# Sums of weights and of x from GpSimd to VectorE in a linear-attention and double-MLP kernel on one core, with later stores

## The chip, the core and the metric

One NeuronCore of a Trainium2 chip runs the whole program. Its engines are TensorE (PE: matmuls; PEld: its weight loads), VectorE (DVE), ScalarE (ACT), GpSimd (POOL) and SyncE (SP), whose queue issues nearly all DMAs here. Each engine takes its instructions in the order of its own queue and waits for the others by semaphores. The metric is the device time of one execution in microseconds (us); less is better.

## The reference

Linear attention with a normalization, then two MLPs, the first gated, the second with softplus, all in float32. The inputs arrive as float64 words.

```python
kv = np.einsum('bhsd,bhse->bhde', k, v)               # 4 x 8 heads, 576 x 64
out = np.einsum('bhsd,bhde->bhse', q, kv)
out = out / np.sqrt(np.mean(out * out, axis=-1, keepdims=True) + 1e-06) * g_norm
x = out.transpose(0, 2, 1, 3).reshape(2304, 512)
x = (x @ w_a) * (x @ w_b) @ w_out                     # 512 -> 1536 -> 512
h = x @ w_in                                          # 512 -> 2048
out = (np.maximum(h, 0) + np.log1p(np.exp(-np.abs(h)))) @ w_out2   # 2048 -> 512
```

## The kernel before

**Numbers.** Every operand of a matmul is held as two halves, a high one in the rounded format fp32r (written by ACT, `half_hi`, line 169) and the rest (written by DVE, `half_lo`, line 172); three matmuls make one product. Raw weights are loaded as pairs of 32-bit words (`w_load`, line 185) and turned into float32 in place: line 193 (DVE) and line 197 (ACT) in `w_begin`, line 202 (DVE) in `w_value`. Then `w_split` makes the two halves.

**Strassen-like products.** Behind its first third the kernel works on pairs of token blocks (of 512 tokens) with seven products in place of eight. These need sums of blocks of weights and of x. `w_sums` makes four sums from two raw tiles, into the second words of those tiles; each is 128x256, and each of the last two needs one of the first two. `x_steps` makes, for two chunks in each of two pairs of blocks, four whole tiles out of the halves (`whole`, line 692) and four sums (`plus`, line 698), all 128x512; between them `cutting` splits the results on ACT and DVE. `g_sums` (lines 935 and 936) makes sums of activations for the last layer. In the kernel before, all of these run on POOL.

**Order.** The attention and twelve slots of the first MLP are written out by hand (`SCRIPT`) and fill about the first 150 us. Behind it the program is a chain of generators; each `yield` is one *point*, mostly six matmuls of 512 columns. Work beside the matmuls is spread over points in jobs: `job_first` (weights of the first MLP for the first pair, with `w_sums`; 8 times), `job_keep` (weights of the second MLP, with `w_sums`; 16 times), `job_out`, and `job_again`, which loads back what `job_first` stored for the second pair. So `w_sums` runs 24 times and makes 96 sums. `x_steps(0)` lies beside the last slots, `x_steps(1)` beside the second half of the first pair's MLP, on tiles that `unpark` loads back from DRAM. `gated` makes the products of the first MLP, four passes of 16 points for the first pair; one pass has 14 groups of six matmuls of 512 columns and two groups of 24 of 256 columns (`first0`). The compiler may reorder what isn't in the hand-written part: an instruction that is ready may be put ahead of earlier ones on its engine.

**Stores.** Split weights that are used again go to DRAM (`keep`, line 517), raw tiles with their sums too (`drop` in `job_first`, line 629). Both are handed to `later` (line 510), which gives the store out so many points afterwards: 12 by default, 16 in `drop`. All big tiles (raw words, halves, operands) come from one pool of 39 buffers of 4 KB a partition. `park` stores the halves of x of two blocks (line 679), at points 1 and 33.

Of the kernel before, what the change touches and what calls it, by code (L numbers as in the profile page):

```python
# [13 lines left out]
ALU = mybir.AluOpType  # L14
# [98 lines left out]
def attention_gated_softplus_kernel(  # L113
# [14 lines left out]
    nc = tc.nc  # L128
# [14 lines left out]
    def t2(shape, dt=F32, what="t2"):  # L143
        return t2pool.tile(shape, dt, tag="t2", name=nm(what))
# [7 lines left out]
    def t4(shape, dt, what):  # L152
        return big.tile(shape, dt, tag="big", name=nm(what))
# [20 lines left out]
    def split(hi, lo, src):  # L174
        half_hi(hi, src)
        half_lo(hi, lo, src)
# [5 lines left out]
    def w_load(item):  # L182
        key, src = item
        t = t4([P, 512, 2], I32, "raw")
        nc.sync.dma_start(out=t, in_=src.bitcast(I32).rearrange("p (n t) -> p n t", t=2))
        raws[key] = t

    def w_begin(item, parts="AB"):
        t = raws[item[0]]
        low = t[:, :, 0]  # L190
        high_f = t.bitcast(F32)[:, :, 1]
        if "A" in parts:
            nc.vector.tensor_scalar(
                out=low, in0=low, scalar1=29, scalar2=None, op0=ALU.logical_shift_right
            )
        if "B" in parts:
            nc.scalar.activation(out=high_f, in_=high_f, func=AF.Prelu, scale=HIGH_SCALE, alpha=SIGN_SCALE)  # L197

    def w_value(item):
        t = raws[item[0]]  # L200
        low, high = t[:, :, 0], t[:, :, 1]
        nc.vector.scalar_tensor_tensor(  # L202
            out=low, in0=high, scalar=3, in1=low, op0=ALU.logical_shift_left, op1=ALU.bitwise_or
        )

    def w_split(item, word=0):
        w = t4([P, 2, 512], F32R, "w")
        split(w[:, 0], w[:, 1], raws[item[0]].bitcast(F32)[:, :, word])
        return w
# [297 lines left out]
    now = [0]  # L507
    due = []

    def later(f, points=12):  # L510
        due.append((now[0] + points, f))
        due.sort(key=lambda x: x[0])

    def keep(key, item, word=0):
        t = w_split(item, word)
        to = kept_w[key] = kept.tile([P, 2, 512], F32, name="kept_" + "_".join(map(str, key)))
        later(lambda: nc.sync.dma_start(out=to, in_=t.bitcast(F32)))
        return t
# [4 lines left out]
        return t  # L523

    def minus(to, a, b):
        nc.gpsimd.tensor_tensor(out=to, in0=a, in1=b, op=ALU.subtract)  # L526

    def w_sums(items, across):
        (l0, h0), (l1, h1) = ([raws[x[0]].bitcast(F32)[:, :, w] for w in range(2)] for x in items)
        k0, k1 = slice(0, 256), slice(256, 512)  # L530
        b11, b12, b21, b22 = l0[:, k0], l0[:, k1], l1[:, k0], l1[:, k1]
        if across:
            b12, b21 = b21, b12
        minus(h0[:, k0], b12, b11)
        minus(h1[:, k0], b22, b12)
        minus(h0[:, k1], b22, h0[:, k0])
        minus(h1[:, k1], b21, h0[:, k1])
# [81 lines left out]
    def job_first(m, fp):  # L619

        l = [((m, f), {"a": w_a, "b": w_b}[m][f]) for f in (2 * fp, 2 * fp + 1)]

        def made(k, item, word):
            w1[fp, m, k] = w_split(item, word)

        def drop(k):
            t = raws.pop(l[k][0])
            to = kept_w["f", m, fp, k] = kept.tile([P, 512, 2], I32, name=f"kept_{m}_{fp}_{k}")
            later(lambda: nc.sync.dma_start(out=to, in_=t), 16)

        return [lambda x=x: w_load(x) for x in l], [
            lambda: w_begin(l[0]),
            lambda: (w_value(l[0]), w_begin(l[1])),
            lambda: made(0, l[0], 0),
            lambda: w_value(l[1]),
            lambda: w_sums(l, True),
            lambda: made(1, l[1], 0),
            lambda: None,
            lambda: (made(2, l[0], 1), drop(0)),
            lambda: (made(3, l[1], 1), drop(1)),  # L640
        ]
# [43 lines left out]
    def x_steps(pair):  # L685
        j1, j2 = PAIRS[pair]
        r = {}

        def whole(j, kk):
            x = xhl[j, kk].bitcast(F32)  # L690
            t = r[j, kk] = t2([P, 512], what="xr")
            nc.gpsimd.tensor_tensor(out=t, in0=x[:, 0], in1=x[:, 1], op=ALU.add)

        def known(name, j, kk, k):
            ops["x", pair, name, k] = xhl.pop((j, kk))

        def plus(to, a, b, op):
            nc.gpsimd.tensor_tensor(out=to, in0=a, in1=b, op=op)

        def cutting(name, kk, src):  # L700
            t = ops["x", pair, name, kk] = t4([P, 2, 512], F32R, "op")
            split(t[:, 0], t[:, 1], src)

        def sums(kk):
            r11, r12, r21, r22 = (r.pop((j, k)) for j in (j1, j2) for k in (kk, kk + 2))
            plus(r22, r21, r22, ALU.add)
            cutting("S1", kk, r22)
            plus(r21, r11, r21, ALU.subtract)
            plus(r11, r22, r11, ALU.subtract)
            cutting("S2", kk, r11)  # L710
            cutting("S3", kk, r21)
            plus(r12, r12, r11, ALU.subtract)
            cutting("S4", kk, r12)

        def names(kk):
            known("A11", j1, kk, kk)
            known("A12", j1, kk + 2, kk)
            known("A22", j2, kk + 2, kk)
            xhl.pop((j2, kk))

        return [x for kk in range(2) for x in (
            lambda kk=kk: (whole(j2, kk), whole(j2, kk + 2)),
            lambda kk=kk: (whole(j1, kk), whole(j1, kk + 2)),
            lambda kk=kk: (sums(kk), names(kk)),
        )]
# [655 lines left out]
```

## Time and profile before

| | |
|---|---|
| median of 3 runs | 867.63 us (866.86 to 867.80) |
| the profiled execution | 868.36 us, of which the trace's span is 866.6 us |
| PE busy | 836.9 us, 97% of the span |
| DVE busy | 666.4 us, 77% |
| ACT busy | 444.3 us, 51% |
| POOL busy | 216.5 us, 25% |
| granted clock of PE, mean | 0.992 |

All times in rows count from the start of the span. A busy share is the time in which an engine executes, with whatever slows the instruction included; for PE it includes time at the lower clock. The granted clock is 1 at 2.4 GHz and 0.5 at 1.2 GHz. A wait is put down to the instruction whose end released it.

### The profile page before, as it was taken

The page shows a single profiled execution, that of the slowest core. Times are in us where ns is not written, and L with a number is a line of the kernel's source. Part 1 is how long each engine was busy: PE and PEld are TensorE (multiplying, and loading weights), DVE is VectorE, ACT ScalarE, POOL GpSimd, SP SyncE. Part 2 cuts the span into 40 slices and gives each one's busy share as a digit, 9 for nine tenths or more (in the row PEclk, how much of TensorE's full clock was granted, in tenths as well). Part 3 has the DMA queues.
Part 4 walks back from the last instruction along what each step waited for, and adds up shares of the span by engine and source line. Part 5 has one row for each costly group of instructions (what it writes and reads, how often), then busy time and mean ns, then how long its engine had stood idle before and what let it go on. Part 6 is the DMA issues. An engine that isn't in the chain of part 4 may idle for free.

```text
span 866.6 us, 12122 instructions
## 1 busy us (share of the span) xinstructions
PE 836.9 (97%) x4204; PEld 692.9 (80%) x4204; DVE 666.4 (77%) x1051; ACT 444.3 (51%) x806; POOL 216.5 (25%) x168
## 2 busy tenths in 40 slices
PE   7999999997999999899999999999999999999998
PEld 5778788886778887778877788877888888887886
DVE  3988773798988789757778956999992767697951
ACT  5799784446656465446664623336560323235630
POOL 0000000884654157411326412331000212111000
PEclk9999999999999999989999999999999999999999
DMA  9993213545877898428699997345488954425941
GB/s 287 318 250 99 93 73 122 193 179 197 284 294 274 275 365 339 167 103 269 234 406 417 344 397 291 120 141 178 160 277 315 387 186 154 146 86 181 320 167 49
DMA packets 81324, 197.92 MB, mean 228 GB/s; under 512 B 7536, under 2 KB 38768, under 8 KB 81264
## 3 DMA queue, kind: packets, MB, share of 16 engines
q1 hardware_dynamic: 81120, 197.16, 64.8%
q8 instruction: 33, 0.54, 0.3%
q14 instruction: 27, 0.22, 0.1%
q10 hardware_dynamic: 144, 0.00, 0.0%
HBM read 142.08 MB, written 55.05 MB: 227 GB/s over the span
## 4 chain that ended last, share of the span: by engine, by line
PE 69%; DVE 14%; DMA 5%; POOL 4%; ACT 4%; issue 4%; SPq 0%; DVEq 0%; POOLq 0%; ACTq 0%
PE acc L1028 17%; PE z L592 4%; PE v L592 4%; PE x L592 4%; PE a L1202 4%; PE acc L429 4%; PE b L1202 4%; DVE w L172 3%; PE acc L862 3%; PE h L1070 3%; POOL raw L526 2%; PE acc L1048 2%; PE y L592 2%; DMA raw<-in_w_out 2%; PE ya L592 2%
## 5 line engine op out<-in xcount | busy, mean ns | idle before, releaser
L1028 PE MATMUL acc<-op,w2o 128*128 128x512 f32 x672 | 153.7, 390 | 1.5 <-DVE op L172 1.5
L1028 PEld LDWEIGHTS acc<-op,w2o 128*128 128x128 f32 x672 | 125.9, 188 | 28.9 <-DVE op L172 2.8
L172 DVE TENSOR_TENSOR w<-raw,w 128x512 fp32r<-128x512 f32 x148 | 121.5, 842 | 28.0 <-ACT w L169 27.5
L526 POOL TENSOR_TENSOR raw<-raw,raw 128x256 f32<-128x256 f32 x56 | 65.7, 1179 | 269.7 <-DVE raw L202 224.9
L169 ACT ACTIVATE w<-raw 128x512 fp32r<-128x512 f32 x148 | 93.7, 670 | 57.8 <-POOL raw L526 23.1
L583 ACT ACTIVATE g<-g 128x512 f32<-128x512 f32 x64 | 39.3, 630 | 100.6 <-DVE g L580 100.5
L172 DVE TENSOR_TENSOR op<-g,op 128x512 fp32r<-128x512 f32 x96 | 63.7, 707 | 4.6 <-ACT op L169 4.5
L429 PE MATMUL acc<-ghl,w 128*128 128x512 f32 (+1 forms) x240 | 57.0, 379 | 3.6 <-ACT y L455 3.4
L197 ACT ACTIVATE raw<-raw 128x512 f32<-128x512 f32 x68 | 45.2, 679 | 29.0 <-DMA raw<-in_w_out 12.1
L862 PE MATMUL acc<-ghl,wo 128*128 128x512 f32 (+1 forms) x288 | 57.3, 357 | 2.3 <-DVE ghl L172 2.0
L169 ACT ACTIVATE op<-g 128x512 fp32r<-128x512 f32 x96 | 53.7, 622 | 8.5 <-DVE op L172 3.6
L862 PEld LDWEIGHTS acc<-ghl,wo 128*128 128x128 f32 x288 | 47.5, 189 | 12.2 <-DVE ghl L172 3.6
L526 POOL TENSOR_TENSOR raw<-raw 128x256 f32<-128x256 f32 x40 | 45.0, 1129 | 47.3 <-DVE raw L202 38.9
L935 POOL TENSOR_TENSOR s<-g 128x512 f32<-128x512 f32 x14 | 19.6, 1397 | 140.5 <-DVE g L585 133.0
L202 DVE SCALAR_TENSOR_TENSOR raw<-raw 128x512 int32<-128x512 int32 x68 | 50.0, 741 | 4.7 <-ACT raw L197 2.6
L429 PEld LDWEIGHTS acc<-ghl,w 128*128 128x128 f32 x240 | 42.5, 195 | 11.3 <-ACT y L455 3.6
L172 DVE TENSOR_TENSOR ghl<-g,ghl 128x512 fp32r<-128x512 f32 (+1 forms) x56 | 46.3, 836 | 5.4 <-ACT ghl L169 5.3
L592 PE MATMUL z<-op,w 128*128 128x512 f32 x192 | 48.9, 390 | 1.3 <-DVE c L603 1.3
L592 PE MATMUL v<-op,w 128*128 128x512 f32 x192 | 49.2, 391 | 0.0
L592 PE MATMUL x<-op,w 128*128 128x512 f32 x192 | 48.3, 389 | 0.0
L169 ACT ACTIVATE ghl<-g 128x512 fp32r<-128x512 f32 (+1 forms) x56 | 33.4, 609 | 23.1 <-DVE g L396 23.1
L862 PE MATMUL acc<-ghl,w 128*128 128x512 f32 x192 | 44.3, 391 | 0.5 <-DVE ghl L172 0.5
(151 smaller groups left out, 1668.2 us busy)
## 6 DMA issues: line engine op xcount, KB each, us to landing
w<-kept SPq DMA_DIRECT2D x80, 512.0 KB, 5.9
kept<-w SPq DMA_DIRECT2D x64, 512.0 KB, 5.8
w2o<-kept SPq DMA_DIRECT2D x112, 256.0 KB, 4.9
raw<-in_w_out SPq DMA_DIRECT2D x28, 512.0 KB, 6.7
kvraw<-in_kv SPq DMA_DIRECT2D x19, 448.0 KB, 10.5
raw<-in_w_in SPq DMA_DIRECT2D x16, 512.0 KB, 5.8
wo<-kept_wo SPq DMA_DIRECT2D x16, 512.0 KB, 9.9
raw<-in_w_a SPq DMA_DIRECT2D x12, 512.0 KB, 6.9
```

Of the source, the lines that this page charges most:

```text
L169: nc.scalar.activation(out=hi, in_=src, func=AF.Copy)
L172: engine.tensor_tensor(out=lo, in0=src, in1=hi, op=ALU.subtract)
L197: nc.scalar.activation(out=high_f, in_=high_f, func=AF.Prelu, scale=HIGH_SCALE, alpha=SIGN_SCALE)
L202: nc.vector.scalar_tensor_tensor(out=low, in0=high, scalar=3, in1=low, op0=ALU.logical_shift_left, op1=ALU.bitwise_or)
L429: nc.tensor.matmul(out=acc[j][i2][:, :n], lhsT=w[:, a, c2], rhs=g[:, c, :n], start=(opens and i == 0 and (j > 0 or i2 % 2 == 0)), stop=(cl ...
L526: nc.gpsimd.tensor_tensor(out=to, in0=a, in1=b, op=ALU.subtract)
L583: nc.scalar.activation(out=to, in_=to, func=AF.Softplus)
L592: nc.tensor.matmul(out=o, lhsT=w[:, a, (2 * k + kk) * P:(2 * k + kk + 1) * P], rhs=x[:, c, :], start=(start and kk == 0 and i == 0), stop= ...
L862: nc.tensor.matmul(out=to, lhsT=w[:, a, i2 * P:(i2 + 1) * P], rhs=x, start=(f == F0 and i == 0 and (b < 2 or i2 % 2 == 0)), stop=(f == F1 ...
L1028: nc.tensor.matmul(out=set_[where][b], lhsT=w[:, a, b * P:(b + 1) * P], rhs=x[:, c, :], start=(opens and cp == 0 and q == 0), stop=(cp == ...
L1070: nc.tensor.matmul(out=h[:, k, :], lhsT=w[:, a, kk * P:(kk + 1) * P], rhs=yhl[0, kk][:, c, :], start=(k == 0 and kk == 0 and q == 0), stop ...
L1202: nc.tensor.matmul(out=live[x, i], lhsT=wt[x, f][:, a, kk * P:(kk + 1) * P], rhs=xhl[j, kk][:, c, :], start=(kk == 0 and k == 0), stop=(kk ...
```

## The change

The sums of weights (`minus` in `w_sums`) and of x (`whole` and `plus` in `x_steps`) are made by DVE in place of POOL. Sums of activations (`g_sums`) stay on POOL. Stores of split weights are given out 20 points later in place of 12, stores of raw tiles with sums 24 in place of 16. Shapes, operands and the rest of the program are the same.

```diff
-    def later(f, points=12):
+    def later(f, points=20):
         due.append((now[0] + points, f))
         due.sort(key=lambda x: x[0])
...
     def minus(to, a, b):
-        nc.gpsimd.tensor_tensor(out=to, in0=a, in1=b, op=ALU.subtract)
+        nc.vector.tensor_tensor(out=to, in0=a, in1=b, op=ALU.subtract)
...
             to = kept_w["f", m, fp, k] = kept.tile([P, 512, 2], I32, name=f"kept_{m}_{fp}_{k}")
-            later(lambda: nc.sync.dma_start(out=to, in_=t), 16)
+            later(lambda: nc.sync.dma_start(out=to, in_=t), 24)
...
             t = r[j, kk] = t2([P, 512], what="xr")
-            nc.gpsimd.tensor_tensor(out=t, in0=x[:, 0], in1=x[:, 1], op=ALU.add)
+            nc.vector.tensor_tensor(out=t, in0=x[:, 0], in1=x[:, 1], op=ALU.add)
...
         def plus(to, a, b, op):
-            nc.gpsimd.tensor_tensor(out=to, in0=a, in1=b, op=op)
+            nc.vector.tensor_tensor(out=to, in0=a, in1=b, op=op)
```

## Rows read from the trace of the kernel before

**Rows 1.** The page: busy us of each engine, share of span, instructions.

```profile
PE 836.9 (97%) x4204; PEld 692.9 (80%) x4204; DVE 666.4 (77%) x1051; ACT 444.3 (51%) x806; POOL 216.5 (25%) x168
```

**Rows 2.** Table by stretch: length, busy us of each engine, clock, DMA share, GB/s.

```profile
150.00:300.00 150.00, 139.70 (x732) 120.02 (x731) 130.89 (x177) 84.38 (x156) 85.01 (x72) 0.98 0.66 238
300.00:372.00 72.00, 67.70 (x313) 55.88 (x313) 61.07 (x84) 36.85 (x68) 36.52 (x20) 0.97 0.73 279
372.00:510.00 138.00, 135.62 (x629) 111.86 (x628) 105.71 (x174) 78.42 (x139) 46.10 (x36) 0.99 0.83 310
```

**Rows 3.** PE's waits from 140 to 372 us: total us, times, longest.

```profile
PE xa L592 <- DVE y L603: 3.8, 1, 3.8
PE acc L429 <- ACT y L455: 3.4, 1, 3.4
PE b L1164 <- DVE g L396: 2.4, 1, 2.4
PE ya L592 <- ACT ya L614: 2.3, 2, 1.6
PE yb L592 <- ACT yb L614: 2.0, 1, 2.0
```

**Rows 4.** The chain of waits, two stretches: start us, us, what.

```profile
195.52 0.32 SPq L517
...
195.89 5.68 DMA raw<-in_w_b
...
217.99 3.38 POOL raw L526 x3
...
341.85 9.50 POOL xr L692
```

**Rows 5.** Timeline, DVE and POOL around 152 us: start us, us, engine, instruction.

```profile
151.97 0.69 DVE L202 SCALAR_TENSOR_TENSOR raw<-raw 128x512 int32<-128x512 int32 x1
...
152.58 0.42 DVE L193 TENSOR_SCALAR raw<-raw 128x512 int32<-128x512 int32 x1
...
152.89 0.86 POOL L526 TENSOR_TENSOR raw<-raw,raw 128x256 f32<-128x256 f32 x1 [150.66 <-DVE raw L202]
153.11 1.19 DVE L202 SCALAR_TENSOR_TENSOR raw<-raw 128x512 int32<-128x512 int32 x1
```

**Rows 6.** POOL's groups, 150 to 370 us: busy us, mean ns, idle before, releasers.

```profile
L526 POOL TENSOR_TENSOR raw<-raw,raw 128x256 f32<-128x256 f32 x33 | 37.1, 1127 | 217.7 <-DVE raw L202 212.2 <-DMA raw<-in_w_b 3.4 <-issue 1.9
L692 POOL TENSOR_TENSOR xr<-x 128x512 f32<-128x512 f32 x16 | 34.5, 2168 | 13.4 <-DMA x<-kept_x 7.1 <-DVE op L172 6.3
L526 POOL TENSOR_TENSOR raw<-raw 128x256 f32<-128x256 f32 x27 | 27.1, 1007 | 0.9
L698 POOL TENSOR_TENSOR xr<-xr,xr 128x512 f32<-128x512 f32 x16 | 24.5, 1529 | 0.8
```

**Rows 7.** DVE's groups of the whole span, two with both inputs in SBUF.

```profile
L476 DVE TENSOR_TENSOR s<-y,y 128x512 f32<-128x512 f32 x4 | 2.6, 682 | 0.0
L172 DVE TENSOR_TENSOR y<-y,y 128x256 fp32r<-128x256 f32 x4 | 1.4, 417 | 0.0
```

**Rows 8.** DVE's five costliest groups, 150 to 370 us.

```profile
L172 DVE TENSOR_TENSOR w<-raw,w 128x512 fp32r<-128x512 f32 x84 | 77.8, 949 | 7.6 <-ACT w L169 7.4
L202 DVE SCALAR_TENSOR_TENSOR raw<-raw 128x512 int32<-128x512 int32 x38 | 29.3, 773 | 4.1 <-ACT raw L197 2.2
L193 DVE TENSOR_SCALAR raw<-raw 128x512 int32<-128x512 int32 x38 | 22.2, 590 | 5.8 <-DMA raw<-in_w_in 2.7 <-DMA raw<-in_w_a 1.3 <-DMA raw<-in_w_b 1.0
L172 DVE TENSOR_TENSOR ghl<-g,ghl 128x512 fp32r<-128x512 f32 x21 | 21.9, 1060 | 3.2 <-ACT ghl L169 3.2
L172 DVE TENSOR_TENSOR op<-xr,op 128x512 fp32r<-128x512 f32 x16 | 13.9, 922 | 7.1 <-ACT op L169 7.1
```

**Rows 9.** SP's issues between 80 and 135 us: start us, us, instruction.

```profile
85.52 44.27 SPq L679 DMA_DIRECT2D kept_x<-x  x8
129.88 1.15 SPq L185 DMA_DIRECT2D raw<-in_w_in  x2
```

## The prediction

> **What bounds the kernel now.** I read the page first: TensorE (PE) is busy 97% of the span [rows 1], so all that any change can win is the time in which PE stands still or runs at the low clock. The table by stretch says where that is: before 150 us no work of the change exists except a few loads, from 150 to 300 us PE is busy 139.70 of 150 us, from 300 to 372 us 67.70 of 72, from 372 to 510 us 135.62 of 138 [rows 2]. Behind 510 us no instruction that moves is left. So the prize lies in 150 to 372 us: 10.3 + 4.3 = 14.6 us of idle PE. Its granted clock is 0.98 and 0.97 there, 1.00 being the level of 2.4 GHz; 0.02 x 150 + 0.03 x 72 = 5.2 us are lost to stretches at the lower level, 1.2 GHz, which lie behind the longest stalls. Together 19.8 us, and with the 2.4 idle us behind 372 us 22.2 us.
>
> PE's waits name the enders: five groups make 13.9 of the 14.6 us, and each ends with VectorE (DVE) or ScalarE (ACT), never with GpSimd (POOL) itself [rows 3]. The chain of waits shows what stood behind these two. At 195.52 us it passes through a store of line 517 on the queue of SyncE (SP), which can go only when DVE has made what is stored, and right behind it through a load of 5.68 us; at 217.99 us three POOL sums take 3.38 us; at 341.85 us one POOL sum alone takes 9.50 us [rows 4]. So POOL is 25% busy on the page [rows 1], yet its work is on the path, partly as latency, partly because it slows DVE. The second is seen in the timeline: the same DVE instruction of line 202 takes 0.69 us with POOL idle, and 1.19 us when a POOL sum has begun 0.22 us before it [rows 5].
>
> **What is removed.** In 150 to 370 us POOL executes 33 + 27 sums of weights (line 526), 16 sums of two halves of x (line 692) and 16 of x (line 698): 37.1 + 27.1 + 34.5 + 24.5 = 123.2 us of POOL [rows 6]. A further 36 sums of weights lie behind 370 us (96 in all by the code, 60 of them here). The sums of line 935 and 936 behind 510 us stay on POOL.
>
> **What is added to DVE.** The trace has no DVE instruction of exactly these sums, but near ones: 128x512 with both inputs in SBUF takes 682 ns, 128x256 takes 417 ns [rows 7]. The stride of two words in the weights' sums is the same that line 172 reads in w<-raw, so I add nothing for it. 60 x 0.417 + 32 x 0.682 = 25.0 + 21.8 = 46.8 us in 150 to 370 us. Durations of neighbours overlap a little in the records, so this is the upper end.
>
> **What DVE gets back.** With POOL quiet, the groups that it slowed fall to their undisturbed durations, 683 ns for the two-input ones of 512 columns (as 682 in [rows 7]), 0.69 us for line 202 and 0.42 us for line 193 [rows 5]. From the means [rows 8]: w 84 x (0.949 - 0.683) = 22.3 us, ghl 21 x (1.060 - 0.683) = 7.9, op 16 x (0.922 - 0.683) = 3.8, line 202 38 x (0.773 - 0.69) = 3.2, line 193 38 x (0.590 - 0.42) = 6.5. Sum 43.7 us. That these means are contention and not a property of the tiles is borne out by the group that has the same instruction elsewhere [rows 7]. So DVE gains 46.8 - 43.7 = +3.1 us: the work comes over nearly for free. Bounds: all of it back and overlapping records, a few us below zero; nothing back, +46.8 us.
>
> DVE is busy 130.89 + 61.07 = 192.0 us of these 222 us [rows 2]; with +3.1 it is 195.1 us. If all 19.8 us came back the stretch would last 202.2 us, and DVE would be 96% full. That is my reason not to count on all of it: an in-order engine at 96% still makes PE wait now and then.
>
> A page of the Trainium skill speaks against the change: "Perfetto Trace Analysis", section Optimizing Scalar/DVE Operations, holds that with a saturated DVE it may pay to give work to ScalarE or even GpSimd, which is the opposite direction. It adds that between DVE and GpSimd this might not help, as they share a read port. By its first half the time would be that of the third rival below; the means of [rows 8] side with the second half.
>
> **New waits.** The weights' sums read what DVE itself wrote one step earlier (line 202), so on DVE they wait for no one; before, POOL waited for DVE, and ACT and the stores of raw weights then for POOL. Four dependent sums last 4 x 0.417 = 1.7 us in place of 3.38 us for three. In the second pair the sums of x read tiles that come back from DRAM: POOL waited 7.1 us for those loads [rows 6]. On DVE whatever is queued behind waits too: the splits of w and ghl, and the evacuations that PE needs. Price 0 to 7.1 us, in the worst case off the gain; I take 0 to 1, since DVE there has a backlog of its own and comes later to them than POOL did.
>
> **The stores.** Line 517's stores are given out 20 points after the split in place of 12, line 629's 24 in place of 16. I take this at zero. Points seem to set a priority, not a time: the eight stores of x of line 679, four given out at point 1 and four at point 33, are all issued from 85.52 to 129.8 us, ahead of the two loads that were given out before all points [rows 9]. What can be won is that a load no longer stands behind a store that waits for DVE, as at 195.5 us [rows 4]; what can be lost is in the second rival.
>
> **The sum**, stall by stall [rows 3]. Those behind POOL work, 2.0 + 2.3 + 3.8 = 8.1 us, go, but for about 1.5 us at 369 us, where DVE has to empty PSUM banks one after the other in any case: 6.6 us. Of the two around 200 us, 2.4 + 3.4 = 5.8 us, I take half, 2.9 us: they are DVE throughput, which hardly changes, plus a late load. The clock gives back in proportion, some 0.7 x 5.2 = 3.7 us. Behind 372 us zero: 36 sums x 0.417 = 15 us come to a DVE that is busy 105.7 of 138 us [rows 2], at most 2.4 us to win and about as much to lose. Total 13.2 us. The profiled execution took 868.36 us (span 866.6); 868.36 - 13.2 = 855.2 us. Its time is 0.73 us above the median of the runs, 867.63, so for a median I say 854.4 us.
>
> **Rivals.** (1) *DVE takes the place of POOL as the limit.* At 96% it still makes PE wait as it does now in 150 to 300 us, and only the stall behind the 9.50 us sum goes, with its share of the clock: about 5 us, 862.7 us. For it: the fullness worked out above. Against: half of the waits are latency through POOL, not throughput.
>
> (2) *The stores hold buffers.* The pool has 39 big tiles, and raw weights, their splits and all operands come out of it. If points do set times, each of the 8 stores of one pass of `gated` frees its tile 8 of 16 points later, that is 4 tiles more in use. A pass has 132 matmuls, at 139.70 / 732 = 0.19 us [rows 2] 25.2 us, four passes 101 us; if tiles set the pace there, 101 x 4 / 39 = 10.3 us are lost, against about 10 us won outside these passes and in them: near 868 us, no change. Against it: in [rows 9] the order goes by what is ready.
>
> (3) *The contention doesn't come back*, because what slows DVE is another user of memory (the loads are dense in the same stretch). Then DVE has 192.0 + 46.8 = 238.8 us to do in 222: +16.8 us, 884.4 us. It decides from the point where less than 16.8 of the 43.7 us come back, 38%. Against it: line 202 in [rows 5], 0.69 or 1.19 us within two microseconds, by POOL alone.
>
> **How the numbers follow.** Forecast 0.60 (845.5 to 861 us), rival 1 0.18 (861 to 865.9), rival 2 0.09, rival 3 or a milder form of it 0.13. The range leaves out rival 3 and part of 2: low end 867.63 - 22.2 = 845.4, say 845.5; high end 866.5, just past rival 1. Faster means by over 0.2%, below 865.9 us, and slower above 869.4 us; less than that a measurement of this kernel can hardly tell from no change. Faster 0.78, same 0.09, slower 0.13.
>
> **What would show it.** Right: no POOL work between 150 and 510 us; w<-raw,w near 0.69 us in that stretch; DVE's busy time in 150 to 360 us about as before; line 592's waits for line 614 and line 603 gone or under 1 us; the clock at 1.00. Wrong: the same means near 0.9 us without POOL (rival 3); PE waiting for DVE in many places of under 1 us each (rival 1); loads of raw weights waiting longer for PE, and the stores really later in SP's order (rival 2).

## The result and the profile after

The changed kernel takes 847.21 us in the median (846.87 to 847.32, 4 runs), the kernel before 867.71 us beside it. The ratio is 0.9759 with a 95% interval of 0.974 to 0.9778: 20.5 us less, where 13.2 us were forecast. The profiled execution took 847.19 us, its span is 845.4 us. First the page, engine by engine; against [rows 1] POOL lost 167.4 us, DVE gained 2.0 us, and PE is busy for 8.2 us less with the same 4204 matmuls.

```profile
PE 828.7 (98%) x4204; PEld 688.3 (81%) x4204; DVE 668.4 (79%) x1179; ACT 444.3 (53%) x806; POOL 49.1 (6%) x40
```

The stretch that holds the moved work does the same 1670 or so matmuls in both kernels. The first row is the kernel before, the second the kernel after, in the columns of [rows 2]; the kernel after is in step with it 20 us earlier at the end.

```profile
150.00:510.00 360.00, 343.01 (x1671) 287.75 (x1670) 297.68 (x433) 199.65 (x361) 167.64 (x128) 0.98 0.74 274
```

```profile
150.00:490.00 340.00, 335.58 (x1672) 283.63 (x1671) 300.11 (x561) 200.43 (x362) 0.00 (x0) 1.00 0.79 286
```

PE's idle time in it falls from 17.0 to 4.4 us, 12.6 us less; its busy time falls by 7.4 us, and the granted clock goes from 0.98 to 1.00, the level of 2.4 GHz throughout. Together 20.0 us, nearly the whole gain. DVE is busy 2.4 us more, with 128 more instructions.

The prediction's own stretch ends at 370 us. Up to there the kernel before did 1039 matmuls, and the kernel after had done as many at 353 us:

```profile
150.00:370.00 220.00, 205.40 (x1039) 174.38 (x1038) 189.96 (x256) 121.22 (x222) 121.53 (x92) 0.98 0.69 253
```

```profile
150.00:353.00 203.00, 200.70 (x1039) 171.60 (x1038) 184.57 (x348) 121.87 (x222) 0.00 (x0) 1.00 0.76 275
```

With the 92 sums that left POOL, DVE is busy 5.4 us less, and 91% of the stretch.

PE's waits from 130 to 510 us in the kernel after, in the columns of [rows 3]:

```profile
PE vb L592 <- DVE g L617: 1.9, 2, 1.2
PE acc L862 <- DVE ghl L172: 1.0, 1, 1.0
PE ya L592 <- ACT ya L614: 0.8, 1, 0.8
PE za L592 <- DVE g L603: 0.2, 1, 0.2
PE acc L862 <- DVE g L617: 0.2, 1, 0.2
```

None of the waits of [rows 3] is left (in the kernel before they end at 198, 204, 223, 250, 276 and 369 us). No wait is over 1.2 us; the two for line 617 are new and end at 262 and 288 us, and the one for line 614 is another, at 416 us.

DVE's groups from 150 to 355 us show where its 47 us of new work went. Columns as in [rows 8]; the four rows of lines 526, 698 and 692 are the moved sums.

```profile
L172 DVE TENSOR_TENSOR w<-raw,w 128x512 fp32r<-128x512 f32 x84 | 55.5, 685 | 5.2 <-ACT w L169 5.1
L202 DVE SCALAR_TENSOR_TENSOR raw<-raw 128x512 int32<-128x512 int32 x39 | 26.7, 690 | 2.5 <-ACT raw L197 1.3
L193 DVE TENSOR_SCALAR raw<-raw 128x512 int32<-128x512 int32 x40 | 16.5, 423 | 4.2 <-DMA raw<-in_w_out 2.0 <-DMA raw<-in_w_in 1.8 <-DMA raw<-in_w_b 0.3
L172 DVE TENSOR_TENSOR ghl<-g,ghl 128x512 fp32r<-128x512 f32 x21 | 14.2, 687 | 1.2 <-ACT ghl L169 1.2
L526 DVE TENSOR_TENSOR raw<-raw,raw 128x256 f32<-128x256 f32 x33 | 13.7, 421 | 0.3
L526 DVE TENSOR_TENSOR raw<-raw 128x256 f32<-128x256 f32 x27 | 11.4, 420 | 0.1
L698 DVE TENSOR_TENSOR xr<-xr,xr 128x512 f32<-128x512 f32 x16 | 11.0, 688 | 0.2
L692 DVE TENSOR_TENSOR xr<-x 128x512 f32<-128x512 f32 x16 | 10.6, 684 | 0.0
L172 DVE TENSOR_TENSOR op<-xr,op 128x512 fp32r<-128x512 f32 x16 | 10.1, 686 | 0.0
```

The sums cost 421, 420, 688 and 684 ns, where 417 and 682 were taken from other lines: 13.7 + 11.4 + 11.0 + 10.6 = 46.7 us. The old groups w, line 202, line 193, ghl and op fell from 949, 773, 590, 1060 and 922 ns [rows 8] to 685, 690, 423, 687 and 686 ns. The sums wait for next to nothing (at most 0.3 us a group); the wait of 7.1 us for x's loads that POOL had [rows 6] has no successor.

### The profile page after: what moved, and what is told of

The parts are those of the page before. It is cut to its first block, busy times and chain, and to the rows that moved or that the text cites. A ratio compares the mean times of both kernels' runs of the same rounds, so it can differ in the third digit from the quotient of the medians.

```text
span 845.4 us, 12022 instructions
## 1 busy us (share of the span) xinstructions
PE 828.7 (98%) x4204; PEld 688.3 (81%) x4204; DVE 668.4 (79%) x1179; ACT 444.3 (53%) x806; POOL 49.1 (6%) x40
## 4 chain that ended last, share of the span: by engine, by line
PE 78%; DVE 10%; DMA 8%; ACT 2%; issue 1%; SPq 0%; DVEq 0%; ACTq 0%
PE acc L1028 18%; PE acc L862 9%; PE acc L429 5%; PE z L592 5%; PE x L592 5%; PE v L592 5%; PE a L1202 4%; PE b L1202 4%; DMA raw<-in_w_out 4%; PE h L1070 3%; PE y L592 2%; PE acc L1048 2%; DVE w L172 2%; DMA raw<-in_w_in 2%; PE a L1164 2%; PE b L1164 2%
## 5 line engine op out<-in xcount | busy, mean ns | idle before, releaser
L172 DVE TENSOR_TENSOR w<-raw,w 128x512 fp32r<-128x512 f32 x148 | 98.2, 685 | 15.8 <-ACT w L169 15.7
L202 DVE SCALAR_TENSOR_TENSOR raw<-raw 128x512 int32<-128x512 int32 x68 | 46.3, 689 | 3.0 <-ACT raw L197 1.8
L429 PEld LDWEIGHTS acc<-ghl,w 128*128 128x128 f32 x240 | 41.3, 189 | 7.4
L862 PE MATMUL acc<-ghl,w 128*128 128x512 f32 x192 | 43.7, 389 | 0.0
L592 PEld LDWEIGHTS z<-op,w 128*128 128x128 f32 x192 | 35.9, 188 | 8.9 <-DVE c L603 1.5
L592 PEld LDWEIGHTS v<-op,w 128*128 128x128 f32 x192 | 36.0, 188 | 7.5
L862 PEld LDWEIGHTS acc<-ghl,w 128*128 128x128 f32 x192 | 36.0, 188 | 7.4
L592 PEld LDWEIGHTS x<-op,w 128*128 128x128 f32 x192 | 35.9, 188 | 7.4
```

What stands on the lines that cost most here:

```text
L172: engine.tensor_tensor(out=lo, in0=src, in1=hi, op=ALU.subtract)
L202: nc.vector.scalar_tensor_tensor(out=low, in0=high, scalar=3, in1=low, op0=ALU.logical_shift_left, op1=ALU.bitwise_or)
L429: nc.tensor.matmul(out=acc[j][i2][:, :n], lhsT=w[:, a, c2], rhs=g[:, c, :n], start=(opens and i == 0 and (j > 0 or i2 % 2 == 0)), stop=(cl ...
L592: nc.tensor.matmul(out=o, lhsT=w[:, a, (2 * k + kk) * P:(2 * k + kk + 1) * P], rhs=x[:, c, :], start=(start and kk == 0 and i == 0), stop= ...
L862: nc.tensor.matmul(out=to, lhsT=w[:, a, i2 * P:(i2 + 1) * P], rhs=x, start=(f == F0 and i == 0 and (b < 2 or i2 % 2 == 0)), stop=(f == F1 ...
```

## Experiments: which part of the change

Theory: the sums are the whole change, because they slow DVE from POOL and because others wait for them there; the stores are worth nothing. Rivals: the stores let loads go earlier, or hold buffers; or one kind of sum is everything.

**The stores alone** (`e1_stores_only`), on the kernel before:

```diff
-    def later(f, points=12):
+    def later(f, points=20):
...
-            later(lambda: nc.sync.dma_start(out=to, in_=t), 16)
+            later(lambda: nc.sync.dma_start(out=to, in_=t), 24)
```

> The kernel before with the later stores alone (20 and 24 points); all sums stay on GpSimd. Theory (points only set a priority among what is ready, the stores are worth nothing by themselves): within 1.7 us of the 867.7 us of before, with PE waits of the same kind near 200, 223 and 366 us. Rival (a load no longer stands behind a store that waits for VectorE, and this is a large part of the gain): 858 us or less. Rival (stores hold buffers longer): 871 us or more, with raw loads issued later.

Measured: 866.89 us beside 868.32 us, ratio 0.9988 (0.997 to 1.0007): no difference that can be told. The waits of SP's queue from 150 to 330 us are of the same kind and size; this row names the stores that wait for the sums of weights on POOL (total us, times, longest).

```profile
SPq L629 <- POOL raw L526: 42.3, 15, 10.5
```

In the kernel before that row stood at 42.5 us for the same 15 times. Eight points more made no difference in this row, and none that can be told in the time.

**The sums alone** (`e2_sums_only`), the changed kernel with 12 and 16 points again:

```diff
-    def later(f, points=20):
+    def later(f, points=12):
...
-            later(lambda: nc.sync.dma_start(out=to, in_=t), 24)
+            later(lambda: nc.sync.dma_start(out=to, in_=t), 16)
```

> The changed kernel with the old points for the stores (12 and 16): all sums of weights and of x on VectorE. Theory (the sums are the whole change): 845.5 to 849 us. Rival (sums and stores are needed together, the stores by themselves being hidden by GpSimd's delay): 851 to 858 us, with loads issued late behind stores and TensorE waits over 1 us between 190 and 260 us.

Measured: 847.51 us (ratio to before 0.9762, 0.9729 to 0.9794), against 847.21 us with the later stores, and inside the range of the first theory. The sums are the change.

**The weights' sums alone** (`e3_weight_sums_only`), on the kernel before:

```diff
     def minus(to, a, b):
-        nc.gpsimd.tensor_tensor(out=to, in0=a, in1=b, op=ALU.subtract)
+        nc.vector.tensor_tensor(out=to, in0=a, in1=b, op=ALU.subtract)
```

> The kernel before with the 96 sums of weights alone on VectorE; x's 32 sums stay on GpSimd, the stores as before. Theory (contention and delay go with the work that is moved): the stalls behind sums of weights (2.0 us near 223 us, 2.3 us near 249 us, their clock) go, the one near 366 us (3.8 us, 3.4 us more by the clock) stays, the two near 200 us become less: 853 to 861 us. Rival (one kind of sum is everything): about 847 us or about 867 us.

Measured: 854.33 us, ratio 0.985 (0.9817 to 0.9882), 14.0 us less. PE's waits from 140 to 520 us; those below the first two rows come to 0.6 us:

```profile
PE xa L592 <- DVE y L603: 2.6, 1, 2.6
PE acc L862 <- DVE ghl L172: 2.6, 3, 1.1
```

From 195 to 230 us PE stands still no more (in the kernel before it was busy 27.01 of these 35 us), while the stall behind x's sums of the second pair is left, and with it the low clock (0.98 in the second row):

```profile
195.00:230.00 35.00, 35.00 (x213) 31.45 (x213) 33.20 (x68) 28.20 (x52) 0.00 (x0) 1.00 0.81 285
300.00:372.00 72.00, 68.20 (x303) 55.78 (x302) 57.79 (x82) 37.56 (x68) 31.76 (x16) 0.98 0.62 228
```

**x's sums alone** (`e4_x_sums_only`), on the kernel before:

```diff
-            nc.gpsimd.tensor_tensor(out=t, in0=x[:, 0], in1=x[:, 1], op=ALU.add)
+            nc.vector.tensor_tensor(out=t, in0=x[:, 0], in1=x[:, 1], op=ALU.add)
...
-            nc.gpsimd.tensor_tensor(out=to, in0=a, in1=b, op=op)
+            nc.vector.tensor_tensor(out=to, in0=a, in1=b, op=op)
```

> The kernel before with x's 32 sums alone on VectorE; the weights' 96 sums stay on GpSimd, the stores as before. Theory: the stall near 366 us goes with its clock (about 6 us), those near 200 us become less, those near 223 and 249 us stay: 855 to 862 us, and with the run of weights' sums alone the two gains add up to about 20 us. Rival (VectorE has no room for them beside a GpSimd that still slows it): 865 us or more.

Measured: 857.13 us, ratio 0.988 (0.985 to 0.9911), 11.2 us less. The picture is the opposite one, PE's first two waits from 140 to 520 us and the same two stretches:

```profile
PE ya L592 <- ACT ya L614: 2.6, 1, 2.6
PE yb L592 <- ACT yb L614: 2.0, 1, 2.0
```

```profile
195.00:230.00 35.00, 31.48 (x190) 27.27 (x188) 32.18 (x48) 25.45 (x49) 17.28 (x16) 1.00 0.63 228
300.00:372.00 72.00, 72.00 (x341) 60.57 (x341) 60.25 (x100) 40.82 (x74) 7.54 (x8) 1.00 0.68 255
```

Both fell inside the forecast's ranges, but their gains come to 14.0 + 11.2 = 25.2 us, more than the 20.8 us of both (868.32 - 847.51): around 200 us, where the kernel before has both kinds of sum on POOL, moving either of them took most of the stalls away. With the weights' sums gone the order changed too: 15 of the x sums of the first pair ran before 150 us, and POOL has no work from 195 to 230 us (0.00 in the row of `e3_weight_sums_only`). So that run doesn't show what x's sums alone would do there.

## Experiments: slowing or delay

What is left open by these is why: because POOL slows DVE, or because ACT and the stores wait for POOL's results; and what the 47 us cost on DVE itself.

**The same work on POOL beside, for no one** (`e5_pool_beside`), on the changed kernel; so also for `whole` and `plus`, with 416 columns:

```diff
         nc.vector.tensor_tensor(out=to, in0=a, in1=b, op=ALU.subtract)
+        nc.gpsimd.tensor_tensor(out=spare[:, :256], in0=to, in1=to, op=ALU.subtract)
```

> The changed kernel, and beside each of the 128 sums on VectorE one sum of two SBUF inputs on GpSimd into a spare tile that nobody reads: 96 of 256 columns, and 32 of 416 (512 do not fit). So GpSimd works about as much as before, but nobody waits for its results. It tells contention from delay. Theory as predicted (both count, and VectorE would now carry its 47 us in 150 to 355 us and the slowing of about 40 us as well): VectorE's mean for w<-raw,w goes from 0.69 back to 0.9 us or more, VectorE becomes full in that stretch, and the time is 860 to 885 us. Rival (only the delay through GpSimd's results counted, the slowing is hidden): under 851 us though the mean is back at 0.9 us.

Measured: 881.91 us, ratio to before 1.0163 (1.0139 to 1.0187): 34.7 us more than the changed kernel, and slower than the kernel before. The time is inside the 860 to 885 us of the theory, and DVE is nearly full; the third sign is missed, as the mean of w<-raw,w reached 833 ns (150 to 355 us) and not 0.9 us. The ghl group is at 1016 ns, and the real sums of weights, too, went from 421 to 536 ns:

```profile
L173 DVE TENSOR_TENSOR w<-raw,w 128x512 fp32r<-128x512 f32 x67 | 54.7, 833 | 2.8 <-ACT w L170 2.8
...
L527 DVE TENSOR_TENSOR raw<-raw,raw 128x256 f32<-128x256 f32 x33 | 17.5, 536 | 0.3
...
L173 DVE TENSOR_TENSOR ghl<-g,ghl 128x512 fp32r<-128x512 f32 x15 | 15.0, 1016 | 0.8 <-ACT ghl L170 0.7
```

```profile
150.00:300.00 150.00, 134.78 (x687) 114.72 (x686) 145.07 (x233) 81.84 (x148) 71.23 (x72) 0.95 0.63 218
```

DVE is busy 145.07 of 150 us and PE gets 687 matmuls done. In this run the spare sum follows the real one on DVE, so it is not the kernel before; it is what the third rival of the prediction describes, the work on DVE and the slowing too. That rival gave 884.4 us.

**No sums at all** (`e8_no_sums`), the changed kernel without the 128 sums; what the matmuls take in their place are other numbers, so its results are others too, and it serves for its time alone:

```diff
     def minus(to, a, b):
-        nc.vector.tensor_tensor(out=to, in0=a, in1=b, op=ALU.subtract)
+        return
...
-            t = r[j, kk] = t2([P, 512], what="xr")
-            nc.vector.tensor_tensor(out=t, in0=x[:, 0], in1=x[:, 1], op=ALU.add)
+            r[j, kk] = x[:, 0]
...
-            nc.vector.tensor_tensor(out=to, in0=a, in1=b, op=op)
+            return
```

> The changed kernel without the 128 sums of weights and of x on any engine (the second words of the raw weights and the high halves of x are used in their place, so part of the products is of other numbers). It gives the floor for this order of work: what is left of TensorE's waits when the sums cost nothing. Theory: VectorE's 47 us in 150 to 355 us cost the changed kernel little, 843 to 847 us, the waits behind 510 us staying. Rival (VectorE's load still costs some us in the changed kernel): 838 to 842 us, less than the waits that are left would allow.

**No sums, but nearly the same work on POOL for no one** (`e9_no_sums_pool_beside`), as `e8` and with sums into a spare tile, of 416 columns where x's sums had 512:

```diff
     def minus(to, a, b):
-        nc.vector.tensor_tensor(out=to, in0=a, in1=b, op=ALU.subtract)
+        nc.gpsimd.tensor_tensor(out=spare[:, :256], in0=a, in1=b, op=ALU.subtract)
...
-            t = r[j, kk] = t2([P, 512], what="xr")
-            nc.vector.tensor_tensor(out=t, in0=x[:, 0], in1=x[:, 1], op=ALU.add)
+            r[j, kk] = x[:, 0]
+            nc.gpsimd.tensor_tensor(out=spare, in0=x[:, 0, :416], in1=x[:, 1, :416], op=ALU.add)
...
-            nc.vector.tensor_tensor(out=to, in0=a, in1=b, op=op)
+            nc.gpsimd.tensor_tensor(out=spare, in0=a[:, :416], in1=b[:, :416], op=op)
```

> As the run without sums, and on GpSimd in the place of each sum one of two SBUF inputs into a spare tile that nobody reads (96 of 256 columns, 32 of 416). VectorE then has the work that it had in the kernel before, GpSimd too, but nobody waits for GpSimd's results. Against the kernel before it tells the delay through GpSimd, against the run without sums the slowing of VectorE. Theory that the slowing is most of the gain: 858 to 868 us, w<-raw,w at 0.9 us in the mean. Theory that the delay is most of it: 843 to 850 us with the same mean. As predicted (8 us of waits behind GpSimd itself, the rest throughput): 853 to 859 us.

Measured: 841.59 us without sums (ratio 0.9693, 0.9675 to 0.9711), 863.13 us with POOL busy beside (0.9944, 0.9927 to 0.996); the kernel before at 868.0 us. Of the two expectations for `e8_no_sums` the theory (843 to 847 us) missed and the rival (838 to 842 us) was met: the sums on DVE do cost the changed kernel some us. The stretch from 150 to 350 us, first without sums, then with POOL beside:

```profile
150.00:350.00 200.00, 200.00 (x1041) 172.33 (x1041) 148.90 (x260) 121.98 (x222) 0.00 (x0) 1.00 0.76 279
```

```profile
150.00:350.00 200.00, 191.82 (x985) 164.17 (x984) 180.46 (x232) 111.17 (x206) 105.40 (x92) 0.98 0.74 268
```

With no sum on any engine PE does not stand still at all. With POOL's 105.40 us beside, of which nobody uses a result, DVE is busy 31.6 us more for 28 instructions fewer, PE waits again, and the clock falls. PE's first three waits of that run are those that ended at 369, 204 and 198 us in the kernel before [rows 3]; here they end at 364, 204 and 197 us:

```profile
PE xa L593 <- DVE y L604: 3.2, 1, 3.2
PE acc L430 <- ACT y L456: 2.9, 1, 2.9
PE b L1165 <- DVE g L397: 2.4, 1, 2.4
```

and the mean of w<-raw,w from 150 to 355 us is 950 ns, where in that stretch the kernel before has 994 ns and the run without sums 686:

```profile
L173 DVE TENSOR_TENSOR w<-raw,w 128x512 fp32r<-128x512 f32 x76 | 70.4, 950 | 4.1 <-ACT w L170 3.8
```

So three differences of medians take the gain apart. `e9` against `e8`, work on POOL for no one: 863.13 - 841.59 = 21.5 us. The kernel before against `e9`, delay through POOL's results: 868.0 - 863.13 = 4.9 us. Against them the sums' own cost on DVE: 847.21 - 841.59 = 5.6 us. 21.5 + 4.9 - 5.6 = 20.8 us, which comes out by construction. Each kernel has an order of its own from the compiler, so a us or two of each term may be due to that.

Is the first term all slowing? Nobody reads the spare tile, but a tile that POOL reads can't be filled anew before POOL is done. The waits in `e9` say where that counted. Up to 380 us no instruction of DVE or ACT waits for POOL, and SP's loads do so for 1.5 us in all. By then `e9` had lost 19 us, at the same count of instructions (first `e8`, then `e9`):

```profile
150.00:361.00 211.00, 211.00 (x1089) 181.45 (x1089) 150.49 (x263) 127.54 (x232) 0.00 (x0) 1.00 0.72 264
```

```profile
150.00:380.00 230.00, 218.67 (x1090) 185.78 (x1089) 198.49 (x263) 126.71 (x233) 108.77 (x96) 0.97 0.67 243
```

Behind 380 us there are waits for POOL again:

```profile
ACT w L170 <- POOL spare L527: 6.2, 1, 6.2
ACT op L170 <- POOL spare L527: 5.7, 1, 5.7
DVE raw L194 <- POOL spare L527: 3.5, 1, 3.5
SPq L523 <- POOL spare L527: 18.2, 2, 9.2
```

So some 19 us are shown as slowing of DVE, and the rest of the 21.5 us can be either. The second term may hold a little slowing, as the shorter sums of x in `e9` slow DVE somewhat less (950 against 994 ns). But it agrees with single waits: those for line 614 at 223, 250 and 276 us in the kernel before, 2.0 + 2.3 us [rows 3], are not in `e9`. They are not in `e3_weight_sums_only` either, and two of them stay in `e4_x_sums_only`, where POOL makes the weights' sums. The theory that the slowing is most of it stands; the predicted middle, 853 to 859 us for the last run, was too low by 4 us.

**The weights' sums twice** (`e7_weight_sums_twice`), on the changed kernel, to see how much room DVE has:

```diff
     def minus(to, a, b):
-        nc.vector.tensor_tensor(out=to, in0=a, in1=b, op=ALU.subtract)
+        for _ in range(2):
+            nc.vector.tensor_tensor(out=to, in0=a, in1=b, op=ALU.subtract)
```

> The changed kernel with each of the 96 sums of weights made twice on VectorE (the same result twice): 60 x 0.42 = 25 us more in 150 to 355 us, 15 us more in 355 to 500 us, without GpSimd. It asks how much room VectorE has left, where the prediction took it to be nearly full. Theory of the prediction (at 96% it makes TensorE wait): VectorE above 97% in 170 to 350 us and 858 us or more. Rival (there is room, since work for weights may slip): 847 to 851 us.

Measured: 857.91 us, 10.7 us more than the changed kernel for 96 x 0.42 = 40 us of DVE instructions; DVE's busy time over the span grew by 30.0 us (698.4 against 668.4), which counts the overlap of neighbouring records once. First the changed kernel, then this one:

```profile
150.00:350.00 200.00, 197.70 (x1026) 169.11 (x1025) 181.57 (x344) 121.87 (x222) 0.00 (x0) 1.00 0.76 277
```

```profile
150.00:350.00 200.00, 192.78 (x984) 163.42 (x984) 189.93 (x390) 119.04 (x213) 0.00 (x0) 0.98 0.73 265
```

At 91% (181.57 of 200 us) DVE costs PE 2.3 us in 200; at 95% it costs 7.2 us and some clock. The time is 0.1 us under what the first theory asked, and DVE is at 96% from 170 to 350 us, below the 97% that it asked; the rival's 847 to 851 us are missed by more. So this settles no more than that: DVE's load counts with about a quarter of itself here (10.7 of 40 us), not with all and not with nothing.

**All sums on DVE** (`e6_all_sums`), the changed kernel with those of `g_sums` too:

```diff
-        nc.gpsimd.tensor_tensor(out=t, in0=a21, in1=a22, op=ALU.add)
-        nc.gpsimd.tensor_tensor(out=a21, in0=a11, in1=a21, op=ALU.subtract)
+        nc.vector.tensor_tensor(out=t, in0=a21, in1=a22, op=ALU.add)
+        nc.vector.tensor_tensor(out=a21, in0=a11, in1=a21, op=ALU.subtract)
```

> The changed kernel with the 32 sums of activations for the last layer on VectorE as well (they follow 490 us; GpSimd then makes no sums). Adds 32 x 0.69 = 22 us to VectorE behind 490 us, and gives back what GpSimd's 47 us there slow it, some 12 us; VectorE is full only in 530 to 600 us, where TensorE waits 2.4 us today. Theory: 846 to 848.5 us, no difference that can be told. Rival (VectorE becomes the limit in 530 to 620 us): 850 us or more. Rival (the 2.4 us go): 844.5 to 845.5 us.

Measured: 846.81 us (ratio to before 0.9746, 0.9723 to 0.977), against 847.21 us: no difference that can be told. From 510 to 620 us, first the changed kernel and then this one, DVE goes from 101.89 to 103.76 us with 13 more instructions, and PE has nearly the same idle time (2.4 and 2.1 us):

```profile
510.00:620.00 110.00, 107.64 (x471) 87.66 (x470) 101.89 (x166) 51.83 (x94) 21.15 (x14) 1.00 0.53 178
```

```profile
510.00:620.00 110.00, 107.94 (x470) 88.87 (x469) 103.76 (x179) 51.07 (x94) 0.00 (x0) 0.98 0.54 180
```

Over the whole span DVE is busy 11.5 us more (679.9 against 668.4 us) for 32 more sums of 0.69 us, 22 us: here about half of the work pays for itself, and the time doesn't change.

## Why the prediction was right, and where its sizes were off

**The exchange on DVE** was right in its parts. In came 46.7 us, where 46.8 were forecast; back came, from the same five groups with the means measured after, 22.2 + 7.8 + 3.8 + 3.2 + 6.3 = 43.3 us, where 43.7 were forecast. The net was lower than +3.1 us: in the prediction's stretch DVE's busy time fell by 5.4 us. A busy time counts the overlap of neighbouring records once; the prediction had named its 46.8 us an upper end for that reason. (The +2.4 us up to 490 us include 36 more sums.) The advice of the Trainium skill ("Perfetto Trace Analysis", Optimizing Scalar/DVE Operations) to relieve a full DVE did not decide here; its remark there on the shared read port agrees with the mean of w<-raw,w: 950 ns in `e9`, 685 ns in the kernel after, where POOL is idle.

**The new waits** for x's loads (0 to 7.1 us) came out at zero, though PE has two new waits of 1.9 us in all for line 617; **the stores** came out at zero, as taken; `e1` and `e2` show the latter from both sides. Rival 2 falls with them. That points only set a priority was argued from one pair of rows and is not shown; shown is that eight points more make no difference in time that can be told. Rival 1, that DVE takes POOL's place as the limit, falls with the result. Rival 3 falls with the mean of 685 ns while the loads went on; what it would have cost `e5` shows, 881.9 us against its 884.4.

**The sum** was too small, 13.2 for 20.5 us, and three of its terms were mis-sized. First, *half* of the two stalls around 200 us (2.9 of 5.8 us): they went whole. Second, *about 1.5 us left at 369 us*: nothing was left there. Less the 1.9 us of new waits, and counted over the whole stretch, PE's idle time fell by 12.6 us where 6.6 + 2.9 = 9.5 us were taken. Third, *some 0.7 x 5.2 = 3.7 us of the clock*: PE's busy time fell by 7.4 us. The table's 0.98 and 0.97 are rounded, the loss behind 372 us was not counted, and the clock came back whole, not in proportion. 3.1 us of idle time and 3.7 us of busy time are nearly what was missing. That the time lies inside the range all the same is owed to its low end, which was the whole prize of 22.2 us: the result is 1.7 us above it.

**The step that was wrong** under the first term is "they are DVE throughput, which hardly changes". DVE's load hardly changed, and yet these stalls went. With DVE about equally full, PE's loss differed by several us. This is the kernel before from 150 to 350 us; the rows of `e9` and of the kernel after for that stretch stand above:

```profile
150.00:350.00 200.00, 189.16 (x970) 161.24 (x969) 175.68 (x233) 110.98 (x204) 115.10 (x88) 0.98 0.71 263
```

DVE is busy 88% of it and PE is idle for 10.8 us; in `e9` it is 90% and 8.2 us, in the kernel after 91% and 2.3 us. So a fullness of DVE doesn't say by itself what PE loses, and "an in-order engine at 96% still makes PE wait" was no ground for halving the term. The stalls around 200 us are there where POOL works beside DVE, used (the kernel before) or not (`e9`), and gone in the kernel after.

**The split between the causes** was off too. The prediction put 8.1 us of waits behind POOL's own work and the other 5.8 us to throughput and a late load. The 2.0 + 2.3 us for line 614 are delay through POOL's results, as said with `e9`. The 3.8 us at 369 us, which the chain led back to the POOL sum of 9.50 us [rows 4], are not, or not mainly: in `e9`, where no one waits for POOL there, 3.2 us of them stand. That a sum on POOL holds up just the DVE instructions that PE needs next, and that a DVE which is as busy with work of its own can be ahead of PE, fits these runs but is argued, not shown instruction by instruction.

What stays open: the split of the 7.4 us between clock and the pipelined ends of matmuls, and how much of the 5.6 us of DVE's load is due to the order that the compiler chose.

## What to carry to other kernels

Before giving elementwise work with two inputs to GpSimd because VectorE looks full, compare the means of VectorE's own instructions with GpSimd busy and idle: here 123 us of GpSimd work made VectorE's instructions 43 us longer, nearly the 47 us that VectorE needed to do that work itself. Busy time doesn't show this, since the slowing counts as busy. Price a stall with the clock that it costs, and take that from PE's busy time rather than from rounded means.

## What the runs showed of the hardware that was not expected

The cost of the slowing depends on what else DVE has to do. Nearly the same unused POOL work cost 21.5 us where DVE had no sums (`e9` against `e8`), and 34.7 us where it had them (`e5` against the changed kernel).

A us by which POOL slows DVE cost more than a us of DVE's own work. Both `e9` and the changed kernel add about the same busy time to the DVE of `e8` (618.5 us over the span): 671.2 and 668.4 us. The first lost 21.5 us, some 19 of them shown as slowing, the second 5.6 us. Own work isn't always that cheap: the doubled sums of `e7` cost 10.7 us for 30.0 us of busy time, on top of a DVE that was at 91% already.

One POOL instruction can last as long as an unbroken run of DVE's instructions beside it. The sum of 9.50 us in [rows 4] began at 341.85 us, and DVE went on from 341.09 to 350.20 us without a gap; it is of the group of line 692, whose mean is 2.17 us [rows 6]; the 16 of that line on DVE took 684 ns in the mean. In `e9` a single sum of 256 columns took 16.36 us, while DVE went from one instruction to the next, mostly with two inputs and most at their undisturbed 0.68 us; the mean of the other group of such sums there is 0.96 us.

```profile
449.87 16.36 POOL L527 TENSOR_TENSOR spare<-raw,raw 128x256 f32<-128x256 f32 x1 [14.00 <-DMA wo<-kept_wo]
```
